# RetNet then ELU-MLP: another order of units, sums and chunk loads in the later token blocks

## The chip, the cores and the metric

The kernel runs on one core of a Trainium2 chip. The metric is the device time of one execution in microseconds (us). Three runs of the kernel before took 649.08, 649.84 and 649.91 us; their median is 649.84 us. The engines are TensorE (PE), its weight loader (PEld), VectorE (DVE), ScalarE (ACT), GpSimd (POOL) and SyncE (SP), whose queue issues all DMAs here. In this trace the instructions of an engine start in the order in which the source issues them to it.

## The reference, cut to what matters

```python
state = gamma * state + k[t] v[t]^T        # per batch and head, 768 steps, 4 x 8 heads, width 64
y[t]  = (1/8) * q[t] @ state
x     = y as (3072 tokens, 512)
h     = x @ w_in                           # 512 x 2048
g     = where(h > 0, h, exp(min(h, 0)) - 1)
out   = g @ w_out                          # 2048 x 512
```

All of it is fp32.

## The kernel before, in words

The 3072 tokens go in six blocks of 512 (`tb` 0 to 5). Block 0 and block 1's first matrix product have paths of their own. Each later block has three kinds of work, woven into one another by hand, since the order of the source is the order on each engine.

*Retention* of the next block, in five steps (`retention_step`): 0 scores and their masks (DVE), 1 state products, 2 and 3 outputs within a half of the block, 4 what is left of the outputs and the scaling into `xb`. It reads four 1 MB chunks, each q, k and v of 128 tokens. `load` issues one chunk on SP's queue into a pool of four buffers; `scale_v` (L285) and `scale_q` (L315) then scale it on POOL, the latter with the table `etab`. In block 1 that table is replaced: `begin_powers_for_q` writes constants and a ramp on POOL (L296, L297, L300, L301), and each further step of it is two ACT activations into `etab` (L304, L305).

*First matrix product* of a block, by Strassen's scheme: three of its seven products stay on one level (`first_one`, products 1, 6 and 5, for four column groups, 1.73 us each on PE), and the four others (M7, M4, M2, M3) are split once more. Such a `unit` has seven products of 8 PE instructions, some 0.89 us each, in the banks `pa`, `pb` and `pd`, and adds its parts by DVE (L912) into the quarters gC11, gC12, gC21 and gC22. ELU of a quarter's part is two ACT activations (L521, L522) into one of three buffers `r`, and one DVE instruction (L525), the ELU end. The ELU ends wait in a list, `later`, and are issued by `pop` or when the list holds four.

*Second matrix product* (`second_twice`): seven outer products in the order ORDER2, each again seven inner ones (L1015). Each inner product reads one 256 KB piece of weights `wq`, fetched by `fetch_small` through a ring of 11 buffers: the fetch for the eleventh product ahead is issued when a product's matmuls are. ACT copies `ms<-pa` (L1023), and DVE adds (`res`, L912). `inputs_of` forms the four sums `ts` that an outer product needs (L884, four DVE instructions), `form` prepares its input quarter (L821, four DVE instructions). `visit` is called at an outer product's "tail", "first", "middle" and "end", and there the retention steps and loads are placed. For outer product number `at`, "end" stands behind its inner products 1, 2, 6, 7 and 5; products 3 and 4 follow behind the first two of the next one.

In the kernel before, the units run in the order M7, M4, M2, M3; blocks 2 to 5 begin the second product with outer product 2 (C21). All four chunks are loaded together at the end of outer product number 5. In block 1 the constants for `etab` are made there ahead of the four loads.

Of the kernel before, what the change touches and what calls it, by code (L numbers as in the profile page):

```python
# [18 lines left out]
def kernel(  # L19
# [788 lines left out]
    ORDER2 = {tb: [1, 2, 3, 7, 6, 5, 4] if tb == 1 else [2, 1, 3, 7, 6, 5, 4] for tb in range(1, NTB)}  # L808
# [19 lines left out]
    UNITS = {7: [("C22", "C12"), ("C21", "C21")], 4: [("C21", "C21")], 2: [("C11", "C11")], 3: [("C12", "C12")]}  # L828
# [3 lines left out]
    for tb in range(1, NTB):  # L832
# [4 lines left out]
        for j in ORDER2[tb]:  # L837
            last = (4, 3) if j == 4 and tb == NTB - 1 else (3, 4)
            mine = [(tb, 1, j, k) for k in (1, 2, 6, 7, 5) + last]
            to_fetch += mine[:2] + before + mine[2:5]  # L840
            before = mine[5:]
# [72 lines left out]
    def unit(tb, j):  # L914
# [36 lines left out]
        yield  # L951
# [5 lines left out]
        else:  # L957
            nc.scalar.copy(m7, pd)
        product(5, pa, False)
# [47 lines left out]
    def second_twice(tb, ts, work, visit):  # L1007
# [81 lines left out]
        def sum_up(j, m):  # L1089

            kept2[j] = m
            if j in (1, 2) and 1 in kept2 and 2 in kept2:
                add(kept2[2], kept2[1], kept2[2])
                store("C11", kept2[2])
# [20 lines left out]
        for at, j in enumerate(ORDER2[tb]):  # L1115
# [250 lines left out]
    def both(work, other):  # L1366
        for w in work:
            w()
        return other

# [16 lines left out]
    def work_of_second(at):  # L1387
        i = lambda j: inputs_of(j, ts)
        return [
            (i(2), []), (i(3), small_part(7)), (i(7), []), (form(6), i(6)), (i(5), small_part(4)), (form(4), i(4)), (next_x(), []),  # L1390
        ][at]

    qpowers = []
    VISITS = [(0, "end"), (2, "middle"), (3, "first"), (4, "end"), (5, "end")]

    def visit_of_second(at, where):
        if (at, where) == (0, "tail"):
            for _ in tail:
                pass
            flush()  # L1400
        if (at, where) in VISITS:
            retention_step(2, VISITS.index((at, where)))
        if (at, where) == (5, "end"):
            qpowers.append(begin_powers_for_q())
            next(qpowers[0])
            for n in range(CPB):
                load(3 * CPB + n)
                scale_v(3 * CPB + n)
        if at == 6:
            next(qpowers[0], None)  # L1410
            if where == "end":
                for m in range(CPB):
                    scale_q(3 * CPB + m)
# [3 lines left out]
    next(tail)  # L1417
    next(tail)
# [3 lines left out]
    for tb in range(2, NTB):  # L1422
# [8 lines left out]
        qa = {0: ps_r.tile([P, 2, TH], FP32, name="qa", tag="r")}  # L1431
# [3 lines left out]
        qa |= {n: bank(x) for n, x in ((1, "b"), (2, "a"), (3, "d"))}  # L1435
# [119 lines left out]
```

## Time and profile before

| what | us |
|---|---|
| median of three runs | 649.84 |
| the profiled execution | 647.05 |
| its span, first to last instruction | 645.3 |
| PE busy | 624.0 (97%) |
| DVE busy | 515.2 (80%) |
| ACT busy | 275.7 (43%) |
| POOL busy | 45.7 (7%) |
| landing of a 1 MB chunk (median of 22) | 9.7 |
| landing of a `wq` piece (median of 309) | 4.2 |

The span leaves 1.75 us of the profiled execution outside it. The landing rows are medians from issue to landing. The profiled execution is 2.8 us shorter than the median of the three runs. PE's starts repeat from block to block: the first `first_one` begins at 339.46 in block 3 and at 442.52 in block 4, so a block takes 103.06 us. In a timeline, a line gives the start, the duration, the engine, the source line, the operation and its tiles; what stands in brackets is how long the engine had been idle and what ended that.

### The profile page before, as it was taken

To read this page: it belongs to the slowest core of one execution; us is meant where nothing else is said; L and a number is where in the kernel's file an instruction comes from. 1 tells how busy PE (TensorE), PEld (TensorE's weight loads), DVE (VectorE), ACT (ScalarE), POOL (GpSimd) and SP (SyncE) were. 2 spreads that over 40 slices of the span, in tenths; PEclk is the share of its full clock that TensorE was granted. 3 is DMA by queue.
4 is the path that set the end of the run, shared out by engine and by line. 5 is a ranking of instruction groups with operands and counts; after the bars stand their busy time and mean duration, and the time that the engine had idled before them with its cause. 6 is when DMAs were issued, how large, how long until landed. Compare 5 with 4: busy or idle time off the path is not lost.

```text
span 645.3 us, 16746 instructions
## 1 busy us (share of the span) xinstructions
PE 624.0 (97%) x6870; PEld 563.8 (87%) x6870; DVE 515.2 (80%) x918; ACT 275.7 (43%) x516; POOL 45.7 (7%) x60
## 2 busy tenths in 40 slices
PE   8999999999999999999999989999999999999997
PEld 6864578888889988988998989999889999899997
DVE  6688799989787888599869399868769886359986
ACT  5897645025531142584122376113267212358311
POOL 1022000000000024000007000004200000000000
PEclk9999999999999999999999999999999999999999
DMA  8698669699378894257889056889345797234794
GB/s 334 235 425 292 188 203 268 190 275 315 114 242 293 291 391 183 71 144 238 279 274 367 30 149 194 258 281 373 130 114 161 218 306 237 94 100 143 247 312 148
DMA packets 80796, 146.85 MB, mean 228 GB/s; under 512 B 6864, under 2 KB 32336, under 8 KB 75472
## 3 DMA queue, kind: packets, MB, share of 16 engines
q1 hardware_dynamic: 80720, 145.78, 68.6%
q8 instruction: 55, 0.90, 0.5%
q14 instruction: 21, 0.17, 0.1%
HBM read 122.42 MB, written 23.33 MB: 226 GB/s over the span
## 4 chain that ended last, share of the span: by engine, by line
PE 82%; DVE 8%; DMA 5%; issue 2%; ACT 2%; POOL 1%; SPq 0%; DVEq 0%; POOLq 0%
PE pa L1015 18%; PE pd L1015 9%; PE pa L788 4%; PE pb L1015 4%; PE pa L927 4%; PE pa L987 3%; PE pa L565 3%; PE pd L987 3%; PE x L655 3%; DMA chunk<-in_qkv_dram 3%; PE pd L927 3%; PE qa L987 2%; PE pb L987 2%; PE pa L655 2%; PE pd L788 2%
## 5 line engine op out<-in xcount | busy, mean ns | idle before, releaser
L1023 ACT COPY ms<-pa 128x128 f32<-128x128 f32 x104 | 27.6, 266 | 139.5 <-PE pa L1015 131.8
L1015 PE MATMUL pd<-ts,wq 128*128 128x128 f32 x552 | 73.4, 276 | 4.1 <-PE pa L1015 3.5
L1015 PE MATMUL pa<-ts,wq 128*128 128x128 f32 x560 | 74.6, 276 | 1.8 <-ACT r L522 1.3
L1015 PEld LDWEIGHTS pd<-ts,wq 128*128 128x128 f32 x552 | 67.2, 192 | 4.9 <-PE pa L1015 4.1
L1015 PEld LDWEIGHTS pa<-ts,wq 128*128 128x128 f32 x560 | 68.1, 192 | 2.8 <-ACT r L522 2.0
L1015 PE MATMUL pa<-gC,wq 128*128 128x128 f32 x480 | 64.3, 277 | 0.7 <-DVE res L912 0.7
L522 ACT ACTIVATE r<-r 128x512 f32<-128x512 f32 x96 | 60.5, 631 | 3.1
L1015 PEld LDWEIGHTS pa<-gC,wq 128*128 128x128 f32 x480 | 58.8, 192 | 1.7 <-DVE res L912 0.9
L912 DVE TENSOR_TENSOR gC<-pb,gC 128x512 f32<-128x512 f32 x20 | 13.4, 687 | 37.7 <-PE pb L927 37.7
L525 DVE SCALAR_TENSOR_TENSOR gC<-r,gC 128x512 f32<-128x512 f32 x64 | 42.1, 685 | 0.0
L884 DVE TENSOR_TENSOR ts<-gC,ts 128x512 f32<-128x512 f32 x60 | 41.3, 688 | 1.0
L521 ACT ACTIVATE r<-gC 128x512 f32<-128x512 f32 x64 | 40.1, 626 | 4.5 <-DVE gC L525 3.7
L884 DVE TENSOR_TENSOR ts<-gC 128x512 f32<-128x512 f32 x60 | 41.0, 684 | 0.0
L912 DVE TENSOR_TENSOR res<-pd,ms 128x128 f32<-128x128 f32 x68 | 19.6, 288 | 26.2 <-PE pd L1015 17.7
L927 PE MATMUL pa<-ts,wq 128*128 128x128 f32 x256 | 34.8, 279 | 1.0 <-ACT m L948 1.0
L927 PEld LDWEIGHTS pa<-ts,wq 128*128 128x128 f32 x256 | 31.1, 192 | 1.7 <-ACT m L948 1.7
L1015 PE MATMUL pb<-gC,wq 128*128 128x128 f32 x240 | 31.7, 275 | 0.0
L315 POOL TENSOR_TENSOR chunk<-chunk,etab 128x512 f32<-128x512 f32 x12 | 18.5, 1551 | 182.4 <-DMA chunk<-in_qkv_dram 91.4
L1015 PEld LDWEIGHTS pb<-gC,wq 128*128 128x128 f32 x240 | 29.2, 192 | 0.0
L285 POOL TENSOR_TENSOR chunk<-chunk,vf 128x512 f32<-128x512 f32 x16 | 22.4, 1397 | 83.4 <-DMA chunk<-in_qkv_dram 78.0
L1045 ACT COPY res<-pa 128x128 f32<-128x128 f32 x34 | 9.0, 265 | 42.2 <-PE pa L1015 41.9
L912 DVE TENSOR_TENSOR res<-res 128x512 f32<-128x512 f32 (+1 forms) x31 | 24.2, 783 | 1.9
(289 smaller groups left out, 1303.8 us busy)
## 6 DMA issues: line engine op xcount, KB each, us to landing
wq<-scratch_dram SPq DMA_DIRECT2D x309, 256.0 KB, 4.2
chunk<-in_qkv_dram SPq DMA_DIRECT2D x22, 1024.0 KB, 9.7
wraw<-in_w_dram SPq DMA_DIRECT2D x15, 1024.0 KB, 6.1
out_dram<-res SPq DMA_DIRECT2D x14, 256.0 KB, 4.8
scratch_dram<-gT SPq DMA_DIRECT2D x12, 256.0 KB, 4.4
scratch_dram<-m SPq DMA_DIRECT2D x12, 192.0 KB, 6.3
scratch_dram<-so SPq DMA_DIRECT2D x4, 512.0 KB, 4.7
scratch_dram<-wi SPq DMA_DIRECT2D x2, 1024.0 KB, 6.2
```

Of the source, the lines that this page charges most:

```text
L285: eng.tensor_tensor(out=v, in0=v, in1=vf[:, i].unsqueeze(2).to_broadcast([C, H, D]), op=ALU.mult)
L521: nc.scalar.activation(e, h, AF.Relu, scale=-1.0)
L522: nc.scalar.activation(e, e, AF.Exp, scale=-1.0)
L525: nc.vector.scalar_tensor_tensor(g, e, -1.0, h, ALU.add, ALU.max)
L655: nc.tensor.matmul(X[j][:, d, :], lhsT=w[j][:, d * P : d * P + P], rhs=x[j], start=(n == 0 and d == 0), stop=at_end, skip_group_check=True,)
L788: nc.tensor.matmul(ps[:, fi, :], lhsT=w[:, fi, j2, :], rhs=x[:, j2, :], start=(begin and fi == 0 and j2 == 0), stop=(j2 == 1), skip_group_ ...
L884: sub = lambda o, x, y: nc.vector.tensor_tensor(out=o, in0=x, in1=y, op=ALU.subtract)
L912: nc.vector.tensor_tensor(out=o, in0=x, in1=y, op=ALU.add)
L927: nc.tensor.matmul(ps[:, f, :], lhsT=lhs[f], rhs=xs[j][k], start=(begin and f == 0), stop=True, skip_group_check=True,)
L987: nc.tensor.matmul(ps[:, fi, :], lhsT=w[:, fi, j2, :], rhs=x[:, j2, :], start=(j == 1 and fi == 0 and j2 == 0), stop=(j2 == 1), skip_group ...
L1015: nc.tensor.matmul(ps, lhsT=w[:, f, :], rhs=ts[j][k][:, f, :], start=(begin and f == 0), stop=(f == 3), skip_group_check=True,)
L1023: nc.scalar.copy(m, ps)
```

## The change

- The units run in the order M2, M7, M4, M3. M2 stands among the `first_one` products of column groups 2 and 3, and its ELU follows at once; its column groups 0 and 1 use the banks `pb` and `pa` in place of others.
- Every block begins its second product with outer product 1 (C11); the sums for its input are formed right behind M2's ELU, and those for C21 move to the end of C11.
- Inside a unit, product 5 and its sums move from before to behind the third `yield`; the pops of the ELU ends move, so that sums of the next unit's banks stand ahead of them.
- Retention steps move: in block 1 to the ends of outer products 0 to 4, in blocks 2 to 4 steps 3 and 4 from the ends of numbers 4 and 5 to those of 3 and 4.
- Chunks are loaded one at a time: behind the end of number 4, the middle and the end of number 5, and the middle of number 6. In block 1 the first `scale_v` now stands ahead of the constants for `etab`, and the activations into `etab` stand in number 5.
- In block 1 the last two products of the first matrix product move behind C11's first two, the last ELU ends behind C11's "middle", and `small_part(7)`, sums of weights for a later unit, from number 1 to number 2.

```diff
-    ORDER2 = {tb: [1, 2, 3, 7, 6, 5, 4] if tb == 1 else [2, 1, 3, 7, 6, 5, 4] for tb in range(1, NTB)}
+    ORDER2 = [1, 2, 3, 7, 6, 5, 4]
...
-    UNITS = {7: [("C22", "C12"), ("C21", "C21")], 4: [("C21", "C21")], 2: [("C11", "C11")], 3: [("C12", "C12")]}
+    UNITS = {2: [("C11", "C11")], 7: [("C22", "C12"), ("C21", "C21")], 4: [("C21", "C21")], 3: [("C12", "C12")]}
...
-        yield
         pd = full(bank("d"))
         product(7, pd, True)
         m7 = new(hpool, "h")
@@
             nc.scalar.copy(m7, pd)
+        yield
         product(5, pa, False)
...
     def work_of_second(at):
         i = lambda j: inputs_of(j, ts)
         return [
-            (i(2), []), (i(3), small_part(7)), (i(7), []), (form(6), i(6)), (i(5), small_part(4)), (form(4), i(4)), (next_x(), []),
+            ([], i(2)), (i(3), []), (i(7), small_part(7)), (form(6), i(6)), (i(5), small_part(4)), (form(4), i(4)),
+            (next_x(), []),
         ][at]
-    qpowers = []
-    VISITS = [(0, "end"), (2, "middle"), (3, "first"), (4, "end"), (5, "end")]
+    qpowers = begin_powers_for_q()
+    LOADS = {(4, "end"): 0, (5, "middle"): 1, (5, "end"): 2, (6, "middle"): 3}
 
     def visit_of_second(at, where):
         if (at, where) == (0, "tail"):
+            next(tail)
+            next(tail)
+        elif (at, where) == (0, "middle"):
             for _ in tail:
                 pass
             flush()
-        if (at, where) in VISITS:
-            retention_step(2, VISITS.index((at, where)))
-        if (at, where) == (5, "end"):
-            qpowers.append(begin_powers_for_q())
-            next(qpowers[0])
-            for n in range(CPB):
-                load(3 * CPB + n)
-                scale_v(3 * CPB + n)
-        if at == 6:
-            next(qpowers[0], None)
-            if where == "end":
-                for m in range(CPB):
-                    scale_q(3 * CPB + m)
+        if where == "end" and at < 5:
+            retention_step(2, at)
+        if at == 5:
+            next(qpowers, None)
+        if (at, where) in LOADS:
+            n = LOADS[at, where]
+            load(3 * CPB + n)
+            scale_v(3 * CPB + n)
+            if n == 0:
+                next(qpowers)
+            for m in [0, 1, 2] if n == 2 else [3] if n == 3 else []:
+                scale_q(3 * CPB + m)
...
-        for n, j in ((0, 6), (1, 6), (0, 5), (1, 5), (2, 1), (3, 1), (2, 6), (3, 6)):
-            first_one(n, j, qa[n])
...
+        for n in (2, 3):
+            qa[n] = ps_r.tile([P, 2, TH], FP32, name="qa", tag="r")
+            first_one(n, 1, qa[n])
+
+        cur = unit(tb, 2)
         next(cur)
+        first_one(2, 6, qa[2])
+        for _ in range(3):
+            next(cur)
+        elu_of(2, 0, 0)
+        elu_of(2, 1, 1)
+        first_one(3, 6, qa[3])
+        next(cur)
+        next(cur, None)
+        pop()
+        elu_of(2, 1, 0)
+        elu_of(2, 0, 1)
+        pop(2)
         first_one(2, 5, qa[2])
+        cur = unit(tb, 7)
+        next(cur)
         first_one(3, 5, qa[3])
+        pop()
+        for w in inputs_of(1, ts):
+            w()
...
             next(tail)
             next(tail, None)
-            elu_of(was, 1, 0)
             next(cur)
-            pop(2)
-            next(cur)
-            elu_of(was, 0, 1)
-            pop()
             next(cur)
             pop()
+            elu_of(was, 1, 0)
+            elu_of(was, 0, 1)
+            next(cur)
+            pop(3)
...
-            elif where == "end" and at in (1, 4, 5) and more:
-                retention_step(tb + 1, {1: 2, 4: 3, 5: 4}[at])
-                for n in range(CPB if at == 5 else 0):
-                    load((tb + 2) * CPB + n)
-                    scale_q((tb + 2) * CPB + n)
-                    scale_v((tb + 2) * CPB + n)
+            elif where == "end" and at in (1, 3, 4) and more:
+                retention_step(tb + 1, {1: 2, 3: 3, 4: 4}[at])
+            if (at, where) in LOADS:
+                m = (tb + 2) * CPB + LOADS[at, where]
+                load(m)
+                scale_q(m)
+                scale_v(m)
```

## The prediction

> **What bounds the kernel now.** I read the page first, then PE's timeline for every place where it sat idle, then the timelines of ACT, DVE and POOL around these places.
>
> ```profile
> PE 624.0 (97%) x6870; PEld 563.8 (87%) x6870; DVE 515.2 (80%) x918; ACT 275.7 (43%) x516; POOL 45.7 (7%) x60
> PE 82%; DVE 8%; DMA 5%; issue 2%; ACT 2%; POOL 1%; SPq 0%; DVEq 0%; POOLq 0%
> ```
>
> PE is the bound: only its idle time can be won, and every new wait of PE is lost in full. The chain of work that ended last says the same. Where PE sits idle (its timeline; the idle time and its releaser are in brackets):
>
> ```profile
> 376.68 1.16 PE L927 MATMUL pa<-ts,wq 128*128 128x128 f32 x8 [0.24 <-ACT m L948]
> 379.98 1.16 PE L927 MATMUL pd<-ts,w_b 128*128 128x128 f32 x8 [1.25 <-DVE h L912]
> 386.79 1.16 PE L927 MATMUL pd<-ts,w_a 128*128 128x128 f32 x8 [0.24 <-DVE h L912]
> 396.36 1.13 PE L1015 MATMUL pa<-ts,wq 128*128 128x128 f32 x8 [0.33 <-ACT r L522]
> 398.36 1.13 PE L1015 MATMUL pd<-ts,wq 128*128 128x128 f32 x8 [0.86 <-PE pa L1015]
> ```
>
> The same five come back in blocks 2 to 5. By starts each costs more than its idle time: products run 0.89 us apart, but 377.67 to 379.98 is 2.31, and the start after a wait comes another 0.10 late. Counted so, a block loses 4.34 us, four blocks 17.4. Two more places are at the end of block 1:
>
> ```profile
> 231.50 0.72 ACT L304 ACTIVATE etab<-r,lng 128x512 f32<-128x512 f32 x1 [2.40 <-DVE xb L429]
> 232.64 0.60 ACT L305 ACTIVATE etab<-r,lng 128x256 f32<-128x256 f32 x1 [0.41 <-DVE xb L429]
> 234.41 0.25 ACT L1023 COPY ms<-pa 128x128 f32<-128x128 f32 x1
> ```
> ```profile
> 233.05 1.16 PE L1015 MATMUL pd<-ts,wq 128*128 128x128 f32 x8 [0.65 <-DVE res L912]
> 234.71 1.16 PE L1015 MATMUL pa<-ts,wq 128*128 128x128 f32 x8 [0.49 <-ACT ms L1023]
> ```
>
> The copy `ms` that PE needed at 234.71 stood behind the `etab` activations, and the first of these had sat waiting until 231.50: what ACT waits for ahead of a copy, PE waits for too. By starts 1.77 us, and 0.71 more at the scores of block 3 (250.05). The last row is POOL beside DVE:
>
> ```profile
> 342.67 1.49 POOL L285 TENSOR_TENSOR chunk<-chunk,vf 128x512 f32<-128x512 f32 x1
> ```
> ```profile
> 343.28 1.42 DVE L912 TENSOR_TENSOR res<-res 128x512 f32<-128x512 f32 x1
> ```
>
> A DVE sum of two SBUF tiles that takes 0.69 alone ends 0.54 after the POOL instruction it overlaps; from 341 to 353 eight of them stretch by some 7.5 us, about 0.95 for each POOL instruction. Nothing on PE waited for them there.
>
> **The units (gain).** I place PE's products after the change at 0.89 and 1.73 us, with u = 0 at `first_one(1, 5)`, and put ACT and DVE behind them with this trace's spacings (DVE 0.60, or 0.72 on the result just before; ACT 0.50 for a copy, 1.20 for a pair of activations). M2 and the start of M7 now have four 1.73 us products among their own: M2's readers end a microsecond early (DVE's `h` at 11.7, its bank is due at 13.1). So the 0.24 before 376.68 and the 1.25 after M7 go. What is late next is DVE behind M7, which has two destinations: from 23.05 it runs eleven instructions without a pause, and M4's `h` ends at 29.96 where the bank `pd` is due at 29.95 (0.06 lost); one ELU end further, `gC` ends at 31.16 for a product due at 30.84 and a refill of 0.10 (0.3). M3's copy `pb` stands behind two activations whose buffer `r` is freed by an ELU end at 30.57: 0.3. M3's copy `m` behind the next pairs: 0.15. At the start of the second product, C11's product 5 ends at 42.8, but its copy waits behind an activation pair until 43.6; then DVE has four sums for C21, two ELU ends and a `res` ahead of the sum that frees `pd`, until 48.36 where product 7 is due at 47.13: 1.3. With four refills of 0.10 a block loses 2.5 instead of 4.34. Bounds of the loss: 0 (298 to 306, where ten products follow each other without a wait) and 4.34 (as before). I take 2.5, which is built from the rows of these very instructions. Four blocks: **-7.4 us**.
>
> **Block 1 (loss).** I follow four queues. The 3rd retention output moves ahead (1.55 us of PE, moved, not added), so product 5 of outer number 4 starts near 218.3 (217.56 before, plus 1.55, less 0.8 from below). DVE then runs the four sums of `small_part(4)` until 222.5; SP's store of them waits for that (it was issued at 221.80 before), and the first chunk's load stands behind it: issued at 222.9. The four 0.6 us sums into `xb` move here too and hold `pd` for 0.45 us. POOL's queue is now: `scale_v` of that chunk, sixteen constants, the ramp, its cast; before, the constants ran at 52 and the ramp at 184, long ahead. And ACT's queue is: first pair into `etab`, a `res` copy, second pair, and the copy `ms` that PE's product 5 of outer number 5 needs. So PE waits for the chunk. Rows:
>
> ```profile
> DMA to landing us min/median/max: 8.2/10.6/12.7
> 183.78 0.55 POOL L300 IOTA r<- 128x512 int32 x1 [130.74 <-DVE gC L525]
> 185.90 1.04 POOL L301 CAST r<-r 128x512 f32<-128x512 int32 x1 [1.56 <-DVE gC L525]
> 235.70 1.04 POOL L285 TENSOR_TENSOR chunk<-chunk,vf 128x512 f32<-128x512 f32 x1 [48.77 <-DMA chunk<-in_qkv_dram]
> ```
>
> The first line is for the four chunks that block 1 loads before. 222.9 + 8.2 lands at 231.1; scale 1.04, constants 1.05 (52.00 to 53.04), ramp 0.55, cast 1.04: 234.8; two pairs and two copies take 231.50 to 234.66 less the 0.41 that they waited, 2.75: 237.6. PE's product is due at 226.3 and starts at 237.75: 11.5 lost. Bounds: the store of 1 MB landed in 5.0, which gives 8.3; the store ahead of the chunk may cost it 2.5 (chunks land 2.5 apart), which gives 14.0. Then the fourth chunk, `scale_v` first, ends on POOL at 254.5 where the scores want it at 253.15 (1.4), and DVE's masks, slowed by six POOL instructions, end 0.7 late for the state products. Sum 0.45 + 11.5 + 1.4 + 0.7 = 14.05, against 1.77 + 0.71 = 2.5 that go. At the start C11's first two products fill the 0.68 that PE waited at 179.24 (0.8 by starts). **+10.8 us**.
>
> [...]
>
> **Blocks 2 and 3 (loss).** T is the start of the next block's first `first_one` (339.46). The four loads were issued 6.6 us before T and the last landed 9.2 after it; POOL's eight instructions then fell where nothing waited. Now the first is issued at T-12.8, behind retention step 4, and its two POOL instructions fall at T-8 to T-2, while DVE does `form(4)` and the sums for C21 in a row. PE's leeway there is 0.4 us (the sum after product 4, ahead of product 7), since the 1.09 us of step 4 moved one outer product ahead. 2 x 0.95 - 0.4 = 1.5 lost. The fourth chunk's load stands in SP's queue behind the fetch that waits for product 7 of outer number 6, T+1.2; 7.9 to land (6.1 for 1 MB of `wraw`, 8.3 for a chunk, nearer to the latter), 1.37 to scale: T+10.5, for scores that want it at T+8.5, now T+10.0: 0.5. Scores come 5.3 us earlier than before, but DVE's list ahead of the masks loses 0.95 to each of six POOL instructions: masks end at T+17.0, and the second half of the state products wants them at 15.7: 1.3. Before, masks ended at 357.48 for state products that began at 357.38, with nothing to spare. Sum 3.3; bounds 0 (as before; PE had no wait here, so nothing can be won) and 5 (a landing 2 us later). Two such places: **+6.6 us**. Block 4 loads nothing. The ring has some ten products of lead and takes the chunk between its fetches; beyond that lead PE would wait for `wq`.
>
> [...]
>
> **At nothing.** The new order of outer products, C11's sum and store one product later, and the moved retention steps 2 and 3: the same instructions on the same engines, with leeway from PE's 1.09 and 1.55 us outputs. If this cover were gone, a DVE sum is 0.6 us a block.
>
> **Sum**: -7.4 + 10.8 + 6.6 = +10.0. The profiled execution, 647.05, becomes 657.05; it lies 2.8 below the median of the runs, so the forecast in their terms is 649.84 + 10.0 = **659.8 us**. A change under 0.2% (1.3 us) can't be told from none.
>
> **Rivals.** (A) Not slower: the `etab` chain is covered. Price 11.5; the rest gives -1.5, 648.3, faster by 0.2%. It decides from a stall of 1.5 us, that is, if ACT's first activation starts by 224.8; for it is POOL's idle time, against it POOL's order, with the chunk issued only at 222.9. 8%. (B) DMA becomes the bound while chunks and `wq` share it: for it the shares of 0.9 to 1.07 around 440 to 454, against it the 20 us afterwards without fetches. Landings 2 us later: 14.0 - 11.5 + 2 x 1.7 + 1 = +6.9, 666.7. 12%. (C) The units gain nothing, for ACT's activation pairs and three `r` buffers take the place of DVE's waits: +7.4, 667.2. Against it, M2's readers have a microsecond. 12%. The forecast itself: 68%.
>
> **How the numbers follow.** Its own range: block 1's stall may miss by -3.2 or +1.5, the two transitions by -3.6 or +3.4 (1.5 to 5 each), the units by -2.6 or +2.4 (-10 to -5); as independent misses (the root of their squares' sum) -5.5 and +4.4: 654.3 to 664.2. B and C reach to 667.2; A and some of the low tail are left out: 653.5 to 667.5. Faster is three quarters of A, 0.06; within 0.2%, 0.03; slower, 0.91.
>
> **What would show it.** One PE wait of 8 to 13 us near 226 to 238 on ACT's `ms`, with ACT idle on POOL's cast and POOL on the first chunk; no wait of 1.25 in the units; a wait near 1.3 at the second product's start; waits on DVE around `form(4)` and on the masks in blocks 2 to 4, none between 4 and 5. Wrong if the `etab` activations start before 226, or if blocks 2 to 5 take as long as before.

## The result and the profile after

The changed kernel takes 669.5 us (median of 4 runs, 668.7 to 671.3), the kernel before 649.5 beside it: ratio 1.032, 95% interval 1.028 to 1.036. It is 20 us slower. The forecast was 659.8 with a range to 667.5: the sign is right, the loss is twice the one foreseen, and the time lies 2.0 above the range.

The page of the kernel after: busy time, the clock granted to PE in 40 slices, and the chain of work that ended last.

```profile
PE 633.4 (95%) x6870; PEld 570.9 (85%) x6870; DVE 510.0 (76%) x918; ACT 274.4 (41%) x516; POOL 44.6 (7%) x60
PEclk9999999999999979999999899999799999999999
PE 69%; DMA 10%; DVE 9%; ACT 7%; issue 3%; POOL 1%; SPq 0%; POOLq 0%; DVEq 0%
```

Two things are new. PE's busy time rose from 624.0 to 633.4 with the same 6870 matmuls, and the clock has slices of 7 and 8. So there is a loss that no wait shows. The chain now runs through DMA for 10% of the span, 5% before.

The profiled execution took 670.15 us against 647.05, +23.1 (the medians differ by 20.1, since that execution of before lies 2.4 under its median here and that of after 0.6 above). Cut at the first `first_one` of each block, the view of busy time by stretch gives the lengths (first column stretch, second length, then PE), of the kernel before and then of the kernel after:

```profile
0.00:235.70 235.70, 230.18 (x2534) 187.70 (x2535) 196.10 (x353) 115.24 (x175) 11.57 (x37) 1.00 0.79 266
235.70:339.46 103.76, 100.37 (x1210) 95.63 (x1209) 82.01 (x143) 41.61 (x89) 10.44 (x8) 1.00 0.65 213
339.46:442.52 103.06, 100.14 (x1195) 95.54 (x1193) 82.03 (x142) 40.44 (x86) 12.03 (x8) 1.00 0.67 219
442.52:545.58 103.06, 100.14 (x1211) 95.54 (x1209) 82.44 (x143) 40.06 (x85) 11.67 (x8) 1.00 0.67 212
545.58:645.28 99.70, 93.13 (x730) 89.42 (x728) 72.61 (x137) 38.37 (x82) 0.00 (x0) 0.99 0.55 176
```
```profile
0.00:245.97 245.97, 232.89 (x2534) 190.21 (x2535) 195.99 (x353) 116.04 (x177) 14.27 (x39) 0.98 0.78 264
245.97:353.02 107.05, 101.07 (x1211) 95.92 (x1209) 81.47 (x143) 40.22 (x86) 10.84 (x9) 1.00 0.62 197
353.02:462.32 109.30, 103.61 (x1194) 97.94 (x1193) 80.28 (x142) 40.20 (x86) 11.29 (x8) 0.97 0.62 205
462.32:570.37 108.05, 102.79 (x1211) 97.51 (x1209) 79.70 (x143) 39.83 (x85) 8.15 (x6) 0.97 0.60 193
570.37:668.21 97.84, 93.02 (x730) 89.37 (x728) 72.59 (x137) 38.14 (x82) 0.00 (x0) 1.00 0.57 181
```

| stretch | before | after | difference | the forecast's terms for it |
|---|---|---|---|---|
| blocks 0, 1 | 235.70 | 245.97 | +10.3 | +9.4 |
| block 2 | 103.76 | 107.05 | +3.3 | +1.0 |
| block 3 | 103.06 | 109.30 | +6.2 | +1.5 |
| block 4 | 103.06 | 108.05 | +5.0 | 0.0 |
| block 5 | 99.70 | 97.84 | -1.9 | -1.8 |

Block 5 holds the units and nothing else of the change: their gain came as forecast. The miss is in blocks 2, 3 and 4, and what stands there is not what the sum had.

**Block 1.** PE's timeline, then ACT's, then POOL's, where the forecast had put a stall of 11.5:

```profile
225.48 1.16 PE L1015 MATMUL pd<-ts,wq 128*128 128x128 f32 x8 [0.24 <-DVE res L912]
236.21 2.08 PE L1015 MATMUL pa<-ts,wq 128*128 128x128 f32 x8 [9.58 <-ACT ms L1023]
238.08 1.91 PE L1015 MATMUL pa<-gC,wq 128*128 128x128 f32 x8
239.79 1.88 PE L1015 MATMUL pb<-gC,wq 128*128 128x128 f32 x8
241.50 1.06 PE L1015 MATMUL pa<-gT,wq 128*128 128x128 f32 x8
```
```profile
233.53 0.72 ACT L304 ACTIVATE etab<-r,lng 128x512 f32<-128x512 f32 x1 [11.57 <-POOL r L301]
...
235.91 0.25 ACT L1023 COPY ms<-pa 128x128 f32<-128x128 f32 x1
```
```profile
230.52 1.04 POOL L285 TENSOR_TENSOR chunk<-chunk,vf 128x512 f32<-128x512 f32 x1 [178.93 <-DMA chunk<-in_qkv_dram]
...
232.89 0.61 POOL L301 CAST r<-r 128x512 f32<-128x512 int32 x1
```

The wait is there with every link foreseen: chunk, scale_v, constants, cast, activations, `ms`. It is 9.58 long instead of 11.5, for the most part since the chunk issued at 223.07 landed in 7.45 instead of 8.2 and the cast took 0.61 instead of 1.04. What was not foreseen comes behind it: three products whose starts lie 1.87, 1.71 and 1.71 apart instead of 0.89, 2.6 us more.

**The scores of the next block.** PE in the first 25 us of block 3, POOL's first instruction on the fourth chunk, there and in block 4, and the issue of that chunk on SP's queue:

```profile
360.08 1.63 PE L339 MATMUL sc<-chunk 64*64 64x64 f32 x96
364.94 1.14 PE L339 MATMUL sc<-chunk 64*64 64x64 f32 x32 [3.23 <-POOL chunk L315]
366.00 3.78 PE L987 MATMUL pa<-xt,w_s 128*128 128x256 f32 x8
369.58 2.70 PE L987 MATMUL pb<-xt,w_b 128*128 128x256 f32 x8
...
475.09 1.13 PE L339 MATMUL sc<-chunk 64*64 64x64 f32 x32 [4.08 <-POOL chunk L315]
```
```profile
363.42 1.46 POOL L315 TENSOR_TENSOR chunk<-chunk,etab 128x512 f32<-128x512 f32 x1 [4.00 <-DMA chunk<-in_qkv_dram]
...
473.77 1.26 POOL L315 TENSOR_TENSOR chunk<-chunk,etab 128x512 f32<-128x512 f32 x1 [3.63 <-DMA chunk<-in_qkv_dram]
```
```profile
353.50 0.33 SPq L109 DMA_DIRECT2D chunk<-in_qkv_dram  x1
...
464.65 0.33 SPq L109 DMA_DIRECT2D chunk<-in_qkv_dram  x1
```

PE waits 3.23 and 4.08 for the fourth chunk (1.56 in block 2), and again the next products are slow: 3.58 between two `first_one` that are 1.73 apart elsewhere. The view by stretch, cut to show it (the last three columns are the granted clock, the busy share of the DMA engines and GB/s):

```profile
360.97:364.38 3.41, 0.74 (x52) 0.60 (x43) 3.34 (x9) 0.00 (x0) 0.96 (x1) 1.00 1.04 401
364.38:371.20 6.82, 6.26 (x44) 5.15 (x45) 3.18 (x5) 0.59 (x1) 1.69 (x2) 0.50 0.13 48
371.20:374.61 3.41, 3.41 (x119) 2.88 (x118) 1.14 (x3) 0.82 (x2) 0.00 (x0) 1.00 0.02 5
```

PE was busy for 0.74 of 3.41 us, and was then granted a clock of 0.50 for 6.82 us. At 0.50, half of PE's busy time in that stretch, 6.26, is lost (estimate): 3.1. The same reading gives 2.6 in block 1 (231.26 to 241.50 at 0.50, PE busy 5.29) and 2.7 in block 4 (473.60 to 480.43, busy 5.34): 8.4 us in all, the largest single term that the forecast had not.

**The rest.** PE's remaining waits in blocks 2 to 5:

```profile
331.02 0.51 PE L453 MATMUL y<-chunk 64*64 64x64 f32 x18 [2.31 <-issue]
...
351.13 1.16 PE L1015 MATMUL pd<-ts,wq 128*128 128x128 f32 x8 [0.43 <-DVE res L912]
...
460.43 1.16 PE L1015 MATMUL pd<-ts,wq 128*128 128x128 f32 x8 [1.27 <-DVE res L912]
...
629.20 1.16 PE L1015 MATMUL pd<-ts,wq 128*128 128x128 f32 x8 [1.09 <-DVE res L912]
```

The last is the wait for which the forecast had 1.3, once in each of four blocks, 1.09 each time; the five waits of a block of before are gone. Those at 351 and 460 are the transitions around `form(4)` (1.4 and 1.7 by starts, with a 0.51 at 349.57; forecast 1.5 each). The first, 2.31 in the middle of step 3 and released by nothing recorded, was in no term.

### The profile page after: what moved, and what is told of

It reads as the page before. It is cut to its first block, busy times and chain, and to the rows that moved or that the text cites. A ratio compares the mean times of both kernels' runs of the same rounds, so it can differ in the third digit from the quotient of the medians.

```text
span 668.2 us, 16750 instructions
## 1 busy us (share of the span) xinstructions
PE 633.4 (95%) x6870; PEld 570.9 (85%) x6870; DVE 510.0 (76%) x918; ACT 274.4 (41%) x516; POOL 44.6 (7%) x60
## 4 chain that ended last, share of the span: by engine, by line
PE 69%; DMA 10%; DVE 9%; ACT 7%; issue 3%; POOL 1%; SPq 0%; POOLq 0%; DVEq 0%
PE pa L1015 13%; DMA chunk<-in_qkv_dram 7%; PE qa L987 6%; PE pd L1015 6%; PE pa L788 4%; PE pa L927 3%; PE pa L565 3%; PE x L655 3%; PE pb L1015 3%; PE pa L987 3%; ACT r L522 3%; ACT r L521 3%; DMA wq<-scratch_dram 2%; DVE gC L912 2%; PE pd L788 2%
## 5 line engine op out<-in xcount | busy, mean ns | idle before, releaser
L1015 PE MATMUL pa<-ts,wq 128*128 128x128 f32 x560 | 75.1, 278 | 10.1 <-ACT ms L1023 9.6
L1015 PEld LDWEIGHTS pa<-ts,wq 128*128 128x128 f32 x560 | 69.0, 194 | 10.5 <-ACT ms L1023 9.8
L884 DVE TENSOR_TENSOR ts<-gC,ts 128x512 f32<-128x512 f32 x60 | 43.0, 716 | 1.0
L884 DVE TENSOR_TENSOR ts<-gC 128x512 f32<-128x512 f32 x60 | 42.7, 712 | 0.1
L912 DVE TENSOR_TENSOR res<-res 128x512 f32<-128x512 f32 (+1 forms) x31 | 25.9, 839 | 11.3 <-ACT res L1045 9.5
L315 POOL TENSOR_TENSOR chunk<-chunk,etab 128x512 f32<-128x512 f32 x12 | 17.6, 1470 | 197.8 <-DMA chunk<-in_qkv_dram 197.8
```

The costliest lines, as they stand in the source:

```text
L884: sub = lambda o, x, y: nc.vector.tensor_tensor(out=o, in0=x, in1=y, op=ALU.subtract)
L912: nc.vector.tensor_tensor(out=o, in0=x, in1=y, op=ALU.add)
L1015: nc.tensor.matmul(ps, lhsT=w[:, f, :], rhs=ts[j][k][:, f, :], start=(begin and f == 0), stop=(f == 3), skip_group_check=True,)
```

## The experiments

Times are medians; the ratio is to runs of the kernel before on the same chip, whose median lay between 648.1 and 649.5. "After" is 669.5, ratio 1.032.

| run | time | ratio, 95% interval | expected |
|---|---|---|---|
| constants_first | 663.3 | 1.022 (1.019 to 1.026) | 664 |
| fill | 662.2 | 1.021 (1.017 to 1.025) | 661 |
| fourth_earlier | 662.5 | 1.021 (1.018 to 1.024) | 656 to 660 |
| units_alone | 661.3 | 1.020 (1.015 to 1.026) | 647, or 655 |
| scores_later | 658.7 | 1.016 (1.011 to 1.020) | 656 |
| mend_together | 647.9 | 0.999 (0.997 to 1.001) | 642 |
| mend_apart | 650.2 | 1.002 (1.000 to 1.004) | 644 |
| loads_alone | 655.8 | 1.009 (1.006 to 1.013) | 651 |
| mend_masks | 647.6 | 1.000 (0.997 to 1.002) | 642 |
| steps_alone | 651.9 | 1.006 (1.004 to 1.008) | 650 to 653 |
| steps_shifted | 656.0 | 1.010 (1.007 to 1.012) | 648 to 652 |
| mend_sums | 646.2 | 0.995 (0.992 to 0.997) | 643 |

The theory: the `ms` wait comes from POOL's order, the scores' waits from scores that stand too early for the fourth chunk, and the half clock from PE's idleness in these waits. The rivals: transfers are the bound, or the slow products have a cause of their own.

### Is it POOL's order, in block 1?

> The changed kernel with one thing put back: in block 1 the constants, the ramp and its cast stand on POOL ahead of the first chunk's scale_v again. By the queue account PE's wait of 9.58 us on `ms` falls to about 1.8 (the activations then wait only for the xb sums, which ended at 225.02; two pairs and two copies take 3.1, so ms ends near 228.1 where PE was ready at 226.4), and the half clock after it (three products of 1.87, 1.71 and 1.71 instead of 0.89: 2.6 us) goes. PE then reaches the scores of block 2 earlier while the fourth chunk's load is issued no sooner before them, so their wait grows from 1.56 to 3 or 4.5, and a half clock of about 2.8 may follow as in blocks 3 and 4. Sum -9.6 - 2.6 + 1.8 + 2.4 + 2.8 = -5.2: 664 us, 659 to 667. By the rival, that the chunk's own transfer or DVE's sums hold ACT, the wait stays and the time with it: 668 to 671.

```diff
             n = LOADS[at, where]
+            if n == 0:
+                next(qpowers)
             load(3 * CPB + n)
             scale_v(3 * CPB + n)
-            if n == 0:
-                next(qpowers)
```

663.3. PE's timeline in this run, at the same product, and at the scores of block 2:

```profile
226.84 1.16 PE L1015 MATMUL pa<-ts,wq 128*128 128x128 f32 x8 [0.49 <-ACT ms L1023]
...
250.45 1.13 PE L339 MATMUL sc<-chunk 64*64 64x64 f32 x32 [2.62 <-POOL chunk L315]
```

The 9.58 became 0.49. The order on POOL was the cause, as the two kernels differ in that alone. Only 6 us come back, as expected, for the scores of block 2 now wait four times (2.12, 0.68, 0.28, 2.62) where they waited 1.56, and the clock is at half from 244.4 to 254.7. Blocks 3 and 4 still have a wait of 3 us and a half clock behind it. The stall had hidden another.

### Is the half clock due to idleness?

> The changed kernel with more work: 42 products of 0.22 us whose result nobody reads stand in front of the product that waits for `ms` in block 1, and 14 such products in front of the fourth chunk's scores in blocks 3 and 4 (they write where the scores are written afterwards). If the granted clock falls to one half because PE was idle in the 9.58, 3.23 and 4.08 us waits, PE stays at full clock and three stretches of half clock go: 2.6 + 3.1 + 2.7 = 8.4 us less, 661 us, with 70 more products. If what makes the products slow there is something else (transfers, POOL, or the chain of copies behind them), they stay slow and the time stays or grows: 669 to 672.

```diff
+            if x and pp and tb > 3:
+                for _ in range(14):
+                    nc.tensor.matmul(
+                        sc[1].rearrange("p x h t -> p (x h t)")[:, TH : TH + P], lhsT=w_a[0][:, 0, 0, 0, :],
+                        rhs=w_a[0][:, 0, 0, 0, :], start=True, stop=True, skip_group_check=True,
+                    )
             score_products(sc, tb, pp, x)
...
+        if (at, where) == (5, "middle"):
+            fill = ps_r.tile([P, P], FP32, name="y", tag="r")
+            for _ in range(42):
+                nc.tensor.matmul(fill, lhsT=w_a[0][:, 0, 0, 0, :], rhs=w_a[0][:, 0, 0, 0, :], start=True, stop=True, skip_group_check=True)
```

662.2: with 70 products more the kernel is 7.3 us faster than after. PE's timeline in block 1 and at block 3's scores (line numbers are shifted by the edit):

```profile
227.41 9.54 PE L1414 MATMUL y<-w_a 128*128 128x128 f32 x84
237.02 1.16 PE L1021 MATMUL pa<-ts,wq 128*128 128x128 f32 x8
238.01 1.06 PE L1021 MATMUL pa<-gC,wq 128*128 128x128 f32 x8
...
362.25 0.69 PE L339 MATMUL sc<-chunk 64*64 64x64 f32 x32 [0.27 <-POOL chunk L315]
362.87 1.99 PE L993 MATMUL pa<-xt,w_s 128*128 128x256 f32 x8
```

In block 1 POOL begins on the chunk at 231.33, where it was 230.52, so the chain that PE waited for is as late as before; but products run 0.89 and 1.73 apart from the first on, and the granted clock (its mean over the execution is 1.0, where after had 0.982) is full up to PE's last product. This tells idleness from the rivals: what was changed is PE's activity. The 7.3 us are not the clock's alone, for the 2.31 of "issue" in block 2 is gone too (its cause is shown below, by steps_shifted), while the scores of block 2 wait 2.41 where they waited 1.56.

### What do the scores wait for?

> The changed kernel with the fourth chunk's load, and its two POOL instructions, at the end of outer product number 5, next to the third's, in blocks 2 to 4. By the account in which the issue time sets the landing, it is issued 6 to 8 us earlier, queues behind the third chunk for up to 2.5, and is scaled some 2 us before the scores want it (T + 8.7): the waits of 3.23 and 4.08 go, and with them the half clock (3.1 and 2.7): -13.1; back come 0 to 1.5 in each of the two blocks from DVE sums that now stand beside POOL. 656 to 660 us. If the transfers are bound by what else is under way, the fourth chunk lands when it did before or a wait for `wq` appears: 667 to 671.

```diff
-            if (at, where) in LOADS:
-                m = (tb + 2) * CPB + LOADS[at, where]
+            loads = {(4, "end"): [0], (5, "middle"): [1], (5, "end"): [2, 3]}
+            for n in loads.get((at, where), []):
+                m = (tb + 2) * CPB + n
```

> The changed kernel with the scores of the next block two products (3.46 us) later, behind product 5 of column group 0, and the state products one product later, behind product 5 of column group 1; all else, block 1's stall and the loads one by one too, as changed. If what costs is that the scores come before the fourth chunk is scaled (it was ready at T + 10.2, T + 11.9 and T + 12.7, T being the start of the block's first first_one; the scores wanted it at T + 8.7 and want it at T + 12.2 now), the waits of 1.56, 3.23 and 4.08 shrink to 0, 0 and 0.5, no half clock follows in blocks 3 and 4 (3.1 and 2.7), and up to 0.5 in each of three places comes back since only one product now stands between scores and state products: -14.2 + 1.0, 656 us, 654 to 658. If the wait only moves on, to the state products or the next readers of the banks, half of this or less: 663 or more.

```diff
-        if more:
-            retention_step(tb + 1, 0)
         first_one(1, 6, qa[1])
         first_one(0, 5, qa[0])
         if more:
-            retention_step(tb + 1, 1)
+            retention_step(tb + 1, 0)
         first_one(1, 5, qa[1])
+        if more:
+            retention_step(tb + 1, 1)
```

Both take the half clock out of blocks 3 and 4, the one by an earlier chunk, the other by later scores (in block 3 the product behind the scores takes 1.99 in both, where after had 3.78): what costs is that the scores come ahead of the chunk, and an earlier issue brings the chunk earlier. That the transfers have no part in it is not shown. In the kernel after, the DMA engines are busy for a share of 0.97 to 1.08 in each 2 us from 350 to 364, and 1.04 in the row at 360.97 above; and in fourth_earlier the fourth chunk, issued at 348.08, 5.6 us ahead of T where it was 0.5 behind it, takes 12 us to land instead of 9.9 (POOL begins on it at 360.21). scores_later wins 10.8 of the 13.2 expected. fourth_earlier wins 7.0 instead of 10 to 13, in part because another wait takes over, 2.3 us in all. Its PE timeline, in blocks 3 and 4:

```profile
367.68 0.33 PE L379 MATMUL kv<-chunk 64*64 64x64 f32 x4 [1.18 <-DVE chunk L350]
...
472.84 0.33 PE L379 MATMUL kv<-chunk 64*64 64x64 f32 x4 [0.59 <-DVE chunk L350]
```

These are the state products behind DVE's masks: the 1.3 of the forecast, which the kernel after doesn't show since its scores waited longer and DVE caught up meanwhile.

### What are the units worth by themselves?

> Only the order of the units, the second product that begins with C11, the moved pops and the place of the scores are kept from the change; block 1's second product, the retention steps 3 and 4 and the four loads together at the end of number 5 are as in the kernel before. By my account each of blocks 2 to 5 gains 1.8 us by the units (-7.2), and the scores, which stand 3.5 us earlier than before, wait for the last of four chunks: landed T + 9.2, scaled T + 10.6, wanted T + 8.7, so 1.9 in each of three places less the 0.7 there before: +5.0. Sum -2.2: 647.3 us, 644 to 650; with a half clock after each of these waits +8 more, 655. If the units gain nothing: 654.5, or 662 with the half clock.

The block 1 code is the one before; in the later blocks:

```diff
-            elif where == "end" and at in (1, 3, 4) and more:
-                retention_step(tb + 1, {1: 2, 3: 3, 4: 4}[at])
-            if (at, where) in LOADS:
-                m = (tb + 2) * CPB + LOADS[at, where]
-                load(m)
-                scale_q(m)
-                scale_v(m)
+            elif where == "end" and at in (1, 4, 5) and more:
+                retention_step(tb + 1, {1: 2, 4: 3, 5: 4}[at])
+            if (at, where) == (5, "end") and more:
+                for n in range(CPB):
+                    load((tb + 2) * CPB + n)
+                    scale_q((tb + 2) * CPB + n)
+                    scale_v((tb + 2) * CPB + n)
```

661.3, worse than either expectation. PE's timeline at the start of block 3:

```profile
355.44 0.69 PE L339 MATMUL sc<-chunk 64*64 64x64 f32 x32 [1.32 <-POOL chunk L315]
358.29 1.13 PE L339 MATMUL sc<-chunk 64*64 64x64 f32 x32 [2.15 <-POOL chunk L315]
359.36 3.78 PE L987 MATMUL pa<-xt,w_s 128*128 128x256 f32 x8
```

I had reckoned with one wait of 1.9 for the last chunk; the scores wait for the third and the last, and in block 2 for all four. In its view of waits PE waits for L315 11.2 us in all. By stretch it is at half clock (0.50) three times, with PE busy for 15.86 us of them, 7.9 lost. 11.2 less the 0.5 of before, plus 7.9, less 7.4 for the units (1.86 in block 5, four times), is 11.2; measured 13.2. So the place of the scores, which comes with the new order of units, costs more than the units win.

### The loads and the steps by themselves

> The kernel before with only the loads one by one and steps 3 and 4 one outer product earlier, in blocks 2 to 4, as in the change; units, second product and block 1 as before, scores at their old place (wanted at T + 14.3). By my account 1.1 (0.5 to 1.5) in each of two places around form(4), nothing at the scores, 0 to 1.3 at the state products: +2.2, ratio 1.0035, 651 us, 649.5 to 653.5. If a long transfer beside the fetches is what costs, 3 us or more in each place and a half clock: 656 or more.

```diff
-            elif where == "end" and at in (1, 4, 5) and more:
-                retention_step(tb + 1, {1: 2, 4: 3, 5: 4}[at])
-                for n in range(CPB if at == 5 else 0):
-                    load((tb + 2) * CPB + n)
-                    scale_q((tb + 2) * CPB + n)
-                    scale_v((tb + 2) * CPB + n)
+            elif where == "end" and at in (1, 3, 4) and more:
+                retention_step(tb + 1, {1: 2, 3: 3, 4: 4}[at])
+            loads = {(4, "end"): 0, (5, "middle"): 1, (5, "end"): 2, (6, "middle"): 3}
+            if (at, where) in loads and more:
+                m = (tb + 2) * CPB + loads[at, where]
+                load(m)
+                scale_q(m)
+                scale_v(m)
```

655.8, +6.1 by its ratio where I expected 2.2 (the profiled execution, 652.7, lies 3.1 under this median). Around `form(4)` the waits are those expected (0.56 and 0.43, then 1.27), but step 3 of block 2 waits 1.29 and block 5's scores 0.63, both "issue". Hence:

> The kernel before with only retention steps 3 and 4 one outer product earlier in blocks 2 to 4, as in the change; the four loads stay together at the end of number 5. It parts the two halves of run loads_alone (+6.1 by its ratio, +5.6 between the profiled executions). If the wait of 1.3 to 2.4 in step 3 of block 2, which nothing recorded ends, belongs to the place of the step among PE's instructions, it is there again, and the time is 1.5 to 4 longer than before; no wait stands around form(4), as no POOL instruction falls there. If both belong to the loads, the time is that of before within 0.7.

```diff
-            elif where == "end" and at in (1, 4, 5) and more:
-                retention_step(tb + 1, {1: 2, 4: 3, 5: 4}[at])
+            elif where == "end" and at in (1, 3, 4, 5) and more:
+                if at < 5:
+                    retention_step(tb + 1, {1: 2, 3: 3, 4: 4}[at])
                 for n in range(CPB if at == 5 else 0):
```

651.9, +3.7: with the loads as before the "issue" waits are there, and none is around `form(4)`. The steps' place alone is enough for them. They are larger in this trace than in that of loads_alone, but the profiled execution, 655.4, is one of the two longest of eight. PE's list of instructions is fetched in 54 pieces of 16 KB (in the kernel after, such fetches start 254 records of PE apart on the mean); this row of the page has them:

```profile
q8 instruction: 54, 0.88, 0.5%
```

In the records of transfers such a fetch starts 2.2 to 2.4 us before PE goes on. To tell a fetch from something in step 3 itself:

> The kernel of run steps_alone with PE's list of instructions shifted: of the products at the very start that nobody reads, the one of 512 columns goes and the 25 small ones become 57, 124 PE instructions more (matmuls and weight loads) in about the same time; nothing else changes. PE's instructions are fetched in pieces of 16 KB (54 of them for 13,740 instructions, 254 a piece), and in eight runs the wait in step 3 of block 2 ended 2.2 to 2.4 after such a fetch began. If these waits come from the fetch, they move with the shift: those at y in blocks 2 and 3 (2.38 and 1.43) and at the scores of block 5's retention (1.46) in steps_alone are gone or stand elsewhere, with the half clock behind the first, and the time is up to 3.7 less, 648 to 652; it may be as long if the new places are as bad. If the waits belong to these instructions themselves (a bank, a semaphore not shown), they stay where they are, and the time with them: 651 to 656.

```diff
-    unread(1, TB)
-    for n in range(25):
+    for n in range(57):
```

The waits of PE on "issue" (total, times, longest), of steps_alone and then of steps_shifted:

```profile
PE y L453 <- issue: 3.8, 2, 2.4
...
PE sc L339 <- issue: 1.5, 1, 1.5
```
```profile
PE y L453 <- issue: 2.3, 1, 2.3
...
PE pb L1015 <- issue: 1.9, 1, 1.9
```

They moved. Those of blocks 2 to 5 are all gone, and blocks 2 to 4 take 103.9, 104.0 and 103.1, where they took 103.8, 103.1 and 103.1 in the kernel before. In place of them stand one of 2.27 in block 0 (at 29.07) and one of 1.91 in block 1 (at 213.32), each followed by 3.41 us of half clock. The early stretch is 10.1 us longer, of which these account for some 7.6 (another 1.45 is a wait for DVE at 9.81), and the time came out worse: the shift was no cure, but the instructions that waited before don't wait now. The traces say more. PE's list has 14,048 records in steps_alone (6870 matmuls, 6870 weight loads, 308 others). The waits of steps_alone stand where 7105, 9153 and 10,433 of them have gone by, those of steps_shifted where 1217 and 4289 have: each is 193 more than a multiple of 256. So are all 30 waits on "issue" of over 0.25 us in the fourteen traces but eight of 0.5 to 0.7 around `form(4)`, and each of the 30 ends 2.2 to 2.6 us after a fetch began. The rival, that they belong to the instructions of step 3, is out. The loads are then what is left of the +6.1, some 2.4, with intervals that overlap.

### A version that beats both?

> The kernel of run units_alone (block 1, steps 3 and 4 and the four loads together as before the change) with two more edits: the scores two products later as in scores_later, and in block 1 POOL takes scale_q between the scale_v instead of behind all four. The scores want the fourth chunk at T + 12.2; in units_alone it was ready at T + 12.4 in blocks 3 and 4, and in block 1's case the interleaved POOL list should end near T + 11.7. So waits of 0 to 0.5 in three places where before had 0.7 once, no half clock, and the units' 1.7 us in each of four blocks: -6.8 + 0.5 = -6.3, a ratio of 0.990 to the kernel before, 642 us, 640 to 645. If the units' gain exists only where PE comes late anyway, or the masks now hold the state products: 647 to 650.

On units_alone, the edit of scores_later, and in block 1:

```diff
             for n in range(CPB):
                 load(3 * CPB + n)
-                scale_v(3 * CPB + n)
+            scale_v(3 * CPB)
+            scale_v(3 * CPB + 1)
...
-                for m in range(CPB):
-                    scale_q(3 * CPB + m)
+                scale_q(3 * CPB)
+                scale_v(3 * CPB + 2)
+                scale_q(3 * CPB + 1)
+                scale_v(3 * CPB + 3)
+                scale_q(3 * CPB + 2)
+                scale_q(3 * CPB + 3)
```

> As mend_together, with steps 3 and 4 one outer product earlier as in the change and the loads one by one in blocks 2 to 4, the fourth next to the third at the end of number 5. By my account it pays 1.1 in each of two places where POOL meets form(4) (0.51 to 0.68 before `pa`, 0.43 before `pd`), and wins nothing, as the scores no longer wait in either: 1 to 3 us longer than mend_together, 644 us. If loading one by one helps (chunks scaled sooner, no burst of four), it is the shorter of the two.

On mend_together, the edit of fourth_earlier, with steps 3 and 4 at the ends of numbers 3 and 4:

```diff
-            elif where == "end" and at in (1, 4, 5) and more:
-                retention_step(tb + 1, {1: 2, 4: 3, 5: 4}[at])
+            elif where == "end" and at in (1, 3, 4) and more:
+                retention_step(tb + 1, {1: 2, 3: 3, 4: 4}[at])
```

mend_together gives the time of before. PE's timeline in block 4 and the stretches around it:

```profile
460.16 0.33 PE L379 MATMUL kv<-chunk 64*64 64x64 f32 x4 [1.42 <-DVE chunk L350]
```
```profile
458.23:461.64 3.41, 1.73 (x67) 1.19 (x68) 3.38 (x8) 0.59 (x1) 0.00 (x0) 1.00 0.20 73
461.64:465.05 3.41, 3.41 (x67) 2.98 (x59) 3.06 (x8) 0.00 (x0) 0.00 (x0) 0.50 0.02 5
```

The state products wait for masks that stand behind sums which POOL slows (in block 3, DVE sums of 128x256 take 1.26 to 1.38 beside POOL's instructions and 0.41 to 0.42 behind the last of them; PE waits 1.25 there, 1.42 here), and a wait of only 1.42, with 0.27 more behind it, was enough for half clock. mend_apart (loads one by one) is about 2 us longer: its `form(4)` waits are 1.27 twice, and an "issue" wait of 2.38 is in step 3. So the DVE list was shortened ahead of the masks:

> As mend_together, with two more edits: the second four sums for M7's inputs (xparts) stand behind the scores' masks on DVE instead of ahead of them, and in block 1 the constants, the first chunk's load and its scale_v stand at number 5's visit named first, about 3 us earlier. In mend_together PE waited 1.25 and 1.42 (and 0.27 each) for DVE's masks, which stood behind eight sums that POOL slowed; four of these, 1.8 us, now come later, so these waits go, and with them the half clock of block 4 (1.7); in block 1's case 0.65 and 0.71 at the scores go. Sum -1.5 - 1.7 - 1.7 - 1.3 = -6.2 against mend_together, some 642 us, ratio to the kernel before 0.990, range 641 to 645. If the moved sums are then late for the first unit or the second one, or the earlier chunk meets the etab activations as in the change, a new wait takes their place: 647 or more.

```diff
         first_one(0, 6, qa[0])
-        next(xparts)
...
             retention_step(tb + 1, 0)
+        next(xparts)
         first_one(1, 5, qa[1])
```

```diff
+        if (at, where) == (5, "first"):
+            qpowers.append(begin_powers_for_q())
+            next(qpowers[0])
+            load(3 * CPB)
+            scale_v(3 * CPB)
         if (at, where) == (5, "end"):
-            qpowers.append(begin_powers_for_q())
-            next(qpowers[0])
-            for n in range(CPB):
+            for n in range(1, CPB):
                 load(3 * CPB + n)
-            scale_v(3 * CPB)
             scale_v(3 * CPB + 1)
```

647.6, nothing won: the wait went one link on, to the state sums behind the four that were moved (PE's timeline, block 4):

```profile
461.86 5.38 PE L987 MATMUL qa<-xb,w_a 128*128 128x256 f32 x16 [1.83 <-DVE chunk L391]
```

> As mend_masks, with the second four sums of xparts one step later on DVE, behind the sums of the state products. In mend_masks the next PE product (qa) waited 0.54, 1.20 and 1.83 for these sums, which stood behind the four; 1.8 us of DVE go from ahead of them, so 0.5 + 1.2 + 1.8 of waits go but for some 0.2 each, and the half clock of block 4 (1.7). Sum -4.6 against mend_masks: 643 us, ratio to the kernel before 0.992, range 641.5 to 646. If the four sums are then late for M7's inputs, or the wait moves on once more: 647 or more.

```diff
             retention_step(tb + 1, 0)
-        next(xparts)
         first_one(1, 5, qa[1])
         if more:
             retention_step(tb + 1, 1)
+        next(xparts)
```

646.2 against 649.2 of the kernel before beside it, ratio 0.995 (0.992 to 0.997): the first version that is faster, with full clock up to 642.4 of 644.0. It keeps the units, the second product that begins with C11 and the moved sums, and drops block 1's new order, the early scores, the early steps and the loads one by one; in block 1 it has the edits of mend_together and mend_masks. Of the units' 7.4 us three are left: 1.7 goes at the scores (0.5 before), 1.0 at the state sums, 1.5 at an "issue" wait.

## Why the prediction was right or wrong

**The units** (-7.4): right. -1.9 in block 5, where they are alone, so -7.4 for four if the others gain as much (the same waits are gone there), and the wait left is 1.09 where 1.3 stood.

**Block 1** (+10.8): the chain of causes is shown by constants_first, and its size, 9.58 for 11.5, lay within the bounds of 8.3 to 14.0 from the rows. Wrong is what follows a wait: I priced a stall at its length, and this one costs 2.6 more at half clock. The 1.4 at block 2's scores came as 1.56; the 0.7 at the masks didn't show.

**Blocks 2 and 3** (+6.6): the 1.5 around `form(4)` was 1.4 and 1.7. The step that failed is "for scores that want it at T+8.5, now T+10.0: 0.5". The leeway of 1.5 that it grants is the loss at `form(4)`, but that loss falls ahead of T and moves T and the load along with it: the scores want the chunk at T+8.7. That is 1.3 of the miss in each place. The rest is the fourth chunk itself: POOL began on it 9.9 and 9.1 after its issue, not 7.9, and it was issued at T+0.5 and T+2.3, not T+1.2. The 7.9 was taken from landings of 6.1 and 8.3, but the chunks that the kernel after loads in these two places land in 7.3 to 10.5, beside full DMA engines (a share of 0.97 to 1.08 from 350 to 364). The waits of 3.23 and 4.08 in place of 0.5 are 6.3 too little. The masks' 1.3 didn't show beside so long a wait; fourth_earlier showed that they are next in line.

**The clock** (no term): 8.4 in blocks 1, 3 and 4, shown by fill. The rows of before had no wait of PE over 1.25 in these blocks and its clock was full throughout (1.00 by stretch), so nothing there gave a price; but the forecast itself put a wait of 11.5 into the kernel and asked nothing about its aftermath. Every half-rate stretch here that PE's work follows lasts a multiple of 3.41 us (10.24, 6.82 and 6.83 in the kernel after), and all begin on one grid per run (there 133.12 and 109.22 apart, 39 and 32 times 3.41); a stretch of 3.41 us on that grid is called a window below. PE need not be idle for a whole window: half rate followed 0.74 busy of 3.41 in the kernel after and 1.73 of 3.41 in mend_together.

**"At nothing"** failed in one item: "the moved retention steps 2 and 3". Step 3's new place brought 2.31 of "issue" in block 2 and, by steps_alone, +3.7 us in the kernel before (2.3 to 5.1): record 7105 of PE's list, 193 more than a multiple of 256, now falls among its products, and in the kernel after PE went on there 2.40 us after the fetch of a 16 KB piece began. "The same instructions on the same engines" left out the fetches of PE's own list. The new order of outer products and C11's sum left no wait.

**Sum.** By the spans the kernel is 22.9 longer, 12.9 more than the forecast's +10.0: clock +8.4, scores of blocks 3 and 4 +6.3, "issue" +2.3, masks -3.3, block 1's stall -1.9; that is 11.8, and 1.1 is not assigned. In the range's own sum the stall's upper miss is put at +1.5, where its bounds, 11.5 and 14.0, give +2.5; the upper end would be 664.7, still short of the measured time. Of the rivals, A and C are out. B had landings 2 us later from full DMA engines: in blocks 3 and 4 both came, a landing 2.0 and 1.2 later and a DMA share near 1. Its longer stall in block 1 did not come, no wait for `wq` came, and an earlier issue took the waits away, so a bound DMA is not what the 20 us are. No rival had the clock.

**Left open:** what makes the fourth chunk's 9 to 10 us. The full DMA engines stand beside it, and other chunks there take as long (10.5 at most), but no run took the other transfers away. What lies between steps_alone and loads_alone, 2.4, is smaller than their intervals can part.

## What to carry to other kernels

Price a foreseen PE wait of two microseconds or more at its length plus up to half of the PE work that follows in the next 3.4 to 7 us: in the kernel after, waits of 3.23 and 4.08 were followed by a clock of 0.50 for 6.8 us, which cost 3.1 and 2.7 (estimates, half of PE's busy time there), and within the wait of 9.58 began one of 10.2 us, which cost 2.6. In fill, work that nobody reads in these waits kept the clock full. Whether it is paid depended on how much of a window on the grid the wait left busy: 1.42 in mend_together left 1.73 of 3.41 us and was followed by half clock, 2.31 in the kernel after left 1.88 of 3.42 and was not, nor was 2.41 in fill. When work is moved earlier, ask where its last input comes from and whether the delay that seems to give it leeway moves that input's issue too. And look for what waits just behind a stall before removing it: in four runs of this study a removed wait came back one link further on.

## What the runs showed that was not expected

- A stretch of half clock (0.50) followed when PE had been idle for about half of a window or more: 1.73 busy of 3.41 us gave it (mend_together), 1.88 busy of 3.42 did not (the kernel after, 326.83 to 330.25). Cut along each run's grid, the fourteen traces have 24 windows at full clock with 1.73 us busy or less, all followed by half clock, and of some 2600 with 1.8 or more none was. Half clock went on behind windows with 2.94 busy or less and ended behind those with 3.06 or more. The boundary may depend on what kind of products fill the rest, which was not tried.
- By these traces PE waited for its own instructions. Retention's 64x64 products follow each other at some 15 ns (64 in 0.98 us), and where one of the places 256 records apart falls among them or just behind, PE waited up to 2.4 us and went on 2.2 to 2.6 us after the fetch of a 16 KB piece began; 124 instructions more at the start of the list moved these waits from blocks 2 to 5 to blocks 0 and 1. So a change of PE's order or count can cost or win several microseconds in places that it doesn't touch: in steps_shifted waits of 2.27 and 1.91 came in blocks 0 and 1, and those of 2.38, 1.43 and 1.46 in blocks 2 to 4 went.
